# A convolution and two matmuls on one core: the start of the kernel reordered, and the two row tiles of the second matmul one sum apart

## The chip, the core and the metric

The kernel runs on one core of one Trainium2 chip. The metric is the device time of one execution in microseconds (us), the median of several runs. The engines of the core are TensorE (PE in the profile, with its weight loads as PEld), VectorE (DVE), ScalarE (ACT), GpSimd (POOL) and SyncE (SP). SP only issues DMA transfers here; POOL issues DMA transfers too.

## The reference

x is 8 rows of 4096 positions of 192 channels. Each channel belongs to one of 8 heads of 24 channels. A head has 7 weights, which go through a softmax; the output at a position is the weighted sum of that position and the six before it (zeros before the start). The result y goes through two matmuls with a leaky ReLU between them.

```python
# conv: w = softmax(weight) per head, over 7 taps
out = np.einsum('hk,bskhg->bshg', w, x_unf)      # x_unf[b,s,k] = x_pad[b, s+k]
# then, for all 32768 tokens
h = y @ w_in                    # 192 -> 2048
g = np.maximum(0.01 * h, h)
return (g @ w_out).astype(np.float32)            # 2048 -> 192
```

## The kernel before

**Tiling.** Two rows of x are worked on together: their channels lie on partitions 0 to 63 and 64 to 127, so that 192 channels are three *chunks* of 64. A *block* is 512 positions of such a pair, thus 1024 tokens; there are 32 blocks. Blocks 0 to 4 are worked on in two halves of 256 positions, which the code calls groups: groups 0 to 9 are these halves, then each of the blocks 5 to 31 is one group (list `groups`). For blocks 0 and 1 the code also counts halves of 256 positions, q = 0 to 3, which are the groups 0 to 3: "half 1" is group 1, "half 2" is group 2.

**Getting x to the engines.** For blocks 2 and up, `load_x` (L79) has POOL issue six DMA transfers that bring x to SBUF in bf16 (`x_bf`, three buffers), and `transpose_x` (L94) has SP issue three DMA transposes, one for each chunk, into `xt` (channels on partitions, positions along the row). For halves 0 to 3 the way is another: SP loads float32 (`load_first`, L110), an engine casts (`cast_first`, L128), PE transposes into PSUM (`transpose_first`, L143) and an engine copies to `xt` (`evac_first`, L157).

**Convolution.** `conv_jobs` makes 21 DVE instructions for a group: for each chunk one multiplication (L176) and six multiply-adds (L182), from `xt` into `yt`. In the first two groups TensorE does chunks 0 and 1 instead, with diagonal weight matrices (`pe_conv_jobs`, L201), and a copy scales the sum into `yt` (L317 on ACT or L207 on DVE).

**First matmul.** `mm1` (L356) fills two PSUM banks: 12 matmuls of 64 x 128 weights, chunk by chunk, the two row pairs at the same time in the two halves of the array; then one ACT instruction (L363) writes the leaky ReLU to `g`. There are two PSUM buffers (`ph`) of two banks for this. A group takes 16 calls (8 for a half block).

**Second matmul.** For each tile of 128 tokens, 16 matmul pairs add up over the 2048 features into one PSUM bank `po` (four such banks, shared with the transposes and the convolution's sums). The 128 feature rows are split in two *row tiles* of 64 rows, which run on the array at the same time but on different sums: `mm2_slot(q)` (L376) issues row tile 0 of slot q and row tile 1 of slot q - LAG, a slot being one of the 16 steps of one tile. LAG is 24 slots, one and a half sums. As both row tiles of one sum write the same bank, the first matmul of row tile 1 of a tile waits for a *seal*: a semaphore from the ACT instruction of the next `mm1` call, by which row tile 0 has left the bank. When row tile 1 ends, `evac_o` copies the sum to `o_sb` (L415; on ACT for blocks 0 to 4, on DVE after) and each second copy has SP issue the store (L418). After the last group the lone slots of row tile 1 are run, and then the last nine tiles with all 128 rows at once.

**Order.** Every queue runs in the order in which the loop at the end of the function emits instructions; nothing is rescheduled. A group has `steps` of two `mm1` calls and `quota` slots (16 slots in most steps, 8 in the steps of block 5, none in group 0); after the slots of a step come some of the convolution jobs of the *next* group (`ahead`, `per` jobs in a step). In blocks 6 and up DVE thus does, in each step, one copy and up to three jobs. `load_x(blk + 3)` and `transpose_x(blk + 2)` are emitted in the last half or the whole of a block, after a quarter and after half of its steps.

Of the kernel before, what the change touches and what calls it, by code (L numbers as in the profile page):

```python
# [9 lines left out]
FP32 = mybir.dt.float32  # L10
BF16 = mybir.dt.bfloat16
# [3 lines left out]
def kernel(  # L15
# [19 lines left out]
    CH = 64  # L35
# [5 lines left out]
    NFC = F // 128  # L41
    NB = S // ST
    NBLK = (B // 2) * NB
    LAG = NFC + NFC // 2
    WQ = 4
    NHALF = 5
    NPEC = 2
# [19 lines left out]

    x_nat, x_bf, xt = {}, {}, {}

    def load_x(blk):  # L70

        if blk >= NBLK:
            return
        rp, st = divmod(blk, NB)
        t = xb_pool.tile([128, NCH, SUB, 2, CH], BF16, name="x_bf")
        src = x[:, st * ST : (st + 1) * ST, :].rearrange("r (s p) d -> r p s d", p=128)
        for c in range(NCH):
            for e in range(2):
                nc.gpsimd.dma_start(  # L79
                    out=t[:, c, :, e, :],  # L80
                    in_=src[2 * rp + e, :, :, c * CH : (c + 1) * CH],
                )
        x_bf[blk] = t

    def transpose_x(blk):

        if blk >= NBLK:
            return
        rp, st = divmod(blk, NB)
        if st == 0:  # L90
            new_xt(rp)
        t = x_bf.pop(blk)
        for c in range(NCH):
            nc.sync.dma_start_transpose(  # L94
                out=xt[rp][:, c, HALO + st * ST : HALO + (st + 1) * ST].rearrange(
                    "p (s k) -> p s k", s=SUB
                ),
                in_=t[:, c, :, :, :].rearrange("p s e k -> p (s e k)"),
            )
# [62 lines left out]
    def conv_jobs(grp, chunks=range(NCH)):  # L162
        blk, t0, T = grp
        rp, st = divmod(blk, NB)
        if blk not in yt:
            yt[blk] = yt_pool.tile([128, NCH, ST], BF16, name="yt")
        y = yt[blk]
        jobs = []
        for c in chunks:
            for k in range(K):  # L170
                a = BASE + k + st * ST + t0
                src = xt[rp][:, c, a : a + T]
                dst = y[:, c, t0 : t0 + T]
                if k == 0:
                    jobs.append(
                        lambda s=src, d=dst, c=c: nc.vector.tensor_scalar_mul(  # L176
                            d, s, wk[:, c, 0:1]
                        )
                    )
                else:  # L180
                    jobs.append(
                        lambda s=src, d=dst, c=c, k=k: nc.vector.scalar_tensor_tensor(  # L182
                            out=d, in0=s, scalar=wk[:, c, k : k + 1], in1=d,
                            op0=mybir.AluOpType.mult, op1=mybir.AluOpType.add,
                        )
                    )
        return jobs
# [60 lines left out]
    def warm(n):  # L248
        for _ in range(n):
            nc.tensor.matmul(  # L250
                out=wa[:, 0, 0:HT], lhsT=zero[:, 0:128], rhs=zero, start=True, stop=True
            )
# [9 lines left out]
        out=w9[:, 0:K], in_=w9[:, 0:K], func=mybir.ActivationFunctionType.Exp,  # L262
        bias=nmax, scale=1.0, accum_out=w9[:, K : K + 1],
    )
    warm(7)
    wps = psum_h.tile([128, 2, ST], FP32, name="wps", tag="ph")
    for c in range(NCH):
        nc.tensor.matmul(  # L268
# [10 lines left out]
    wkh = const_pool.tile([128, NCH, K], BF16, name="wkh")  # L279
    wkl = const_pool.tile([128, NCH, K], FP32, name="wkl")  # L280
    nc.vector.tensor_copy(out=wkh, in_=wraw[:, :, 0:K])
    nc.vector.tensor_sub(wkl, wraw[:, :, 0:K], wkh)


    diag = [const_pool.tile([128, 2, K, CH], BF16, name=f"diag{c}") for c in range(NPEC)]
# [14 lines left out]
        return act  # L300

    transpose_first(0)
    warm(3)
    diag_high(0)
    diag_low(0, range(2))
    evac_first(0, nc.vector.tensor_copy, nc.scalar.copy)
# [12 lines left out]
        )  # L319

    load_first(2, low)
    for job in conv_jobs(groups[0], range(NPEC, NCH)):
        job()
    for c in range(NPEC):
        pe_jobs, evac_y = pe_conv_jobs(groups[0], c)
        for job in pe_jobs:
            job()
        evac_y(act_scale)
        warm(3)
    cast_first(1, 0, nc.vector.tensor_copy)  # L330
    cast_first(1, 1, nc.vector.tensor_copy)
    load_first(3)
    load_x(2)
    transpose_x(2)


    g, po, osb, seal = {}, {}, {}, {}
# [8 lines left out]
    def mm1(grp, u):  # L346
        blk, t0, T = grp
        y = yt[blk]
        nf = ST // T
        ph = psum_h.tile([128, 2, ST], FP32, name="ph", tag="ph")  # L350
        for i in range(nf):
            f = nf * u + i
            for c in range(NCH):
                for e in range(2):
                    ps = slice(e * CH, (e + 1) * CH)
                    nc.tensor.matmul(  # L356
                        out=ph[:, e, i * T : (i + 1) * T],
                        lhsT=w_in[ps, c, f * 128 : (f + 1) * 128],
                        rhs=y[ps, c, t0 : t0 + T],
                        start=(c == 0),  # L360
                        stop=(c == NCH - 1),
                    )
        act = nc.scalar.activation(  # L363
            out=g[blk][:, nf * u : nf * (u + 1), :, t0 : t0 + T],
            in_=ph.rearrange("p e (i t) -> p i e t", i=nf),
            func=mybir.ActivationFunctionType.Prelu, alpha=0.01,
        )
        while unsealed:
            seal[unsealed.pop()] = act.ins.name

    def mm2_one(rt, m, fc):
        b, e, s = subs[m]
# [35 lines left out]
    def evac_o(n):  # L408
# [7 lines left out]
        if n % 2 == 1:  # L416
# [3 lines left out]
                in_=osb.pop(n // 2),  # L420
            )

    slot, avail = 0, 0
    for i, grp in enumerate(groups):
        blk, t0, T = grp
        steps = T // 64
        if t0 == 0:
            g[blk] = g_pool.tile([128, NFC, 2, ST], BF16, name="g", tag="g")
        quota = (avail - slot) // steps

        if i == 0:
            ahead, pe_ahead = [], []
        elif i == 1:
            ahead = early[4:]
        else:
            ahead = conv_jobs(groups[i + 1]) if i + 1 < len(groups) else []
        per = -(-len(ahead) // (steps - 1)) if T == ST else -(-len(ahead) // steps)
        for j in range(steps):
            for u in range(2 * j, 2 * j + 2):
                mm1(grp, u)  # L440
                if i == 0 and u == 1:
                    transpose_first(1)
                    evac_first(1, nc.vector.tensor_copy, nc.vector.tensor_copy)
                    ahead = conv_jobs(groups[1], range(NPEC, NCH))
                    evacs = []
                    for c in range(NPEC):
                        pe_jobs, evac_y = pe_conv_jobs(groups[1], c)
                        pe_ahead += pe_jobs
                        evacs.append(evac_y)
                    per = len(ahead)  # L450
                if i == 0 and u == 2:
                    for e in range(2):
                        cast_first(2, e, nc.scalar.copy)
                if i == 0 and u == 4:
                    transpose_first(2)
                    evacs[0](act_scale)
                if i == 0 and u in (3, 5):
                    for job in pe_ahead[: 4 * K]:
                        job()
                    pe_ahead = pe_ahead[4 * K :]  # L460
                if i == 1 and u in (0, 2):
                    cast_first(3, u // 2, nc.scalar.copy)
            for _ in range(quota):
                mm2_slot(slot)
                slot += 1
            if i == 0 and j == 3:
                evac_first(2, nc.vector.tensor_copy, nc.vector.tensor_copy)
                early = conv_jobs(groups[2])
                for job in early[:4]:
                    job()  # L470
                evacs[1](nc.vector.tensor_scalar_mul)
# [12 lines left out]
        avail += 2 * T // 128 * NFC  # L484
    while slot < LAST * NFC + LAG:
# [36 lines left out]
```

## Time and profile before

| | us |
|---|---|
| median of 10 runs | 698.71 |
| lowest and highest run | 698.20, 700.07 |
| the profiled execution's own time | 698.33 |
| its span in the profile | 696.6 |
| TensorE matmuls busy | 690.2 |
| VectorE busy | 538.3 |
| ScalarE busy | 513.5 |
| GpSimd busy | 142.0 |

The span is what the profile covers of an execution; the execution's own time has 1.7 us more around it. The first mm1 matmul starts at 12.01; groups 1, 2, 3 and 4 start at 23.12, 34.11, 44.63 and 55.15; block 5 starts at 118.27, block 6 at 134.90, and the last step of block 31 starts at 677.52.

The lines of the timeline below have the start, then the time in us, the engine, the line of the code, the operation, output and inputs, and how many instructions are merged; in brackets is the time that the engine stood idle before, and what ended it. PE matmuls overlap each other, so that the time of a merged line runs a little past the start of the next.

### The profile page before, as it was taken

To read this page: it belongs to the slowest core of one execution; us is meant where nothing else is said; L and a number is where in the kernel's file an instruction comes from. 1 tells how busy PE (TensorE), PEld (TensorE's weight loads), DVE (VectorE), ACT (ScalarE), POOL (GpSimd) and SP (SyncE) were. 2 spreads that over 40 slices of the span, in tenths; PEclk is the share of its full clock that TensorE was granted. 3 is DMA by queue.
4 is the path that set the end of the run, shared out by engine and by line. 5 is a ranking of instruction groups with operands and counts; after the bars stand their busy time and mean duration, and the time that the engine had idled before them with its cause. 6 is when DMAs were issued, how large, how long until landed. Compare 5 with 4: busy or idle time off the path is not lost.

```text
span 696.6 us, 26058 instructions
## 1 busy us (share of the span) xinstructions
PE 690.2 (99%) x11786; PEld 613.2 (88%) x11786; DVE 538.3 (77%) x991; ACT 513.5 (74%) x579; POOL 142.0 (20%) x198
## 2 busy tenths in 40 slices
PE   9999999999999999999999999999999999999997
PEld 6899999678888888888888888888888888888887
DVE  6899999768777787777787777787777787777712
ACT  6888888977777777777777777777777777777770
POOL 6342221320222220222210222211222220000000
PEclk9999999999999999999999999999999999999999
DMA  9996554853656544556645556635556644122112
GB/s 176 123 96 79 82 78 78 88 77 75 74 66 92 82 69 82 73 67 93 81 67 81 73 70 92 81 65 84 68 76 86 85 72 70 55 52 58 47 37 69
DMA packets 184847, 54.39 MB, mean 78 GB/s; under 512 B 148384, under 2 KB 184736, under 8 KB 184736
## 3 DMA queue, kind: packets, MB, share of 16 engines
q0 software_dynamic: 98768, 14.17, 30.5%
q1 hardware_dynamic: 85968, 38.56, 23.0%
q8 instruction: 92, 1.51, 0.9%
q14 instruction: 19, 0.16, 0.1%
HBM read 29.88 MB, written 25.17 MB: 79 GB/s over the span
## 4 chain that ended last, share of the span: by engine, by line
PE 97%; DMA 1%; ACT 1%; POOL 0%; issue 0%; DVE 0%; SPq 0%; POOLq 0%; ACTq 0%
PE po L376 49%; PE ph L356 47%; DMA x_nat<-in_x_dram 1%; ACT g L363 1%; PE acc L201 0%; PE wps L268 0%; ACT diag L296 0%; POOL sel L228 0%; PE warm L250 0%; PE ptr L143 0%; ACT x_bf L128 0%; ACT xt L157 0%; POOL sel L226 0%; DVE o_sb L415 0%; POOL ident masks.py:199 0%
## 5 line engine op out<-in xcount | busy, mean ns | idle before, releaser
L363 ACT ACTIVATE g<-ph 128x1024 bf16<-128x1024 f32 x512 | 496.5, 1021 | 161.0 <-PE ph L356 161.0
L182 DVE SCALAR_TENSOR_TENSOR yt<-xt,wk,yt 128x512 bf16<-128x512 bf16 (+1 forms) x642 | 439.6, 685 | 17.4
L376 PE MATMUL po<-w_out,g 64*128 64x192 bf16 (+1 forms) x8048 | 398.0, 243 | 0.1
L376 PEld LDWEIGHTS <-g 64*128 64x128 bf16 (+1 forms) x8048 | 372.1, 94 | 29.0 <-ACT g L363 0.4
L356 PE MATMUL ph<-yt,w_in 64*128 64x512 bf16 (+1 forms) x3552 | 391.7, 347 | 1.4 <-ACT g L363 1.1
L356 PEld LDWEIGHTS <-w_in 64*128 64x128 bf16 x3552 | 250.0, 94 | 45.8 <-issue 4.8
L79 POOL DMA_DIRECT2D x_bf<-in_x_dram x180 | 133.7, 773 | 431.1 <-DMA xt<-x_bf 422.7
L415 DVE COPY o_sb<-po 128x192 f32<-128x192 f32 x216 | 77.2, 357 | 129.6 <-PE po L376 127.2
L176 DVE TENSOR_SCALAR yt<-xt,wk 128x512 bf16<-128x512 bf16 (+1 forms) x107 | 35.9, 336 | 1.0 <-DMA xt<-x_bf 0.7
L415 ACT COPY o_sb<-po 128x192 f32<-128x192 f32 x40 | 13.1, 327 | 0.0
L201 PE MATMUL acc<-xt,diag 64*64 64x256 bf16 x112 | 8.2, 303 | 0.0
L201 PEld LDWEIGHTS <-diag 64*64 64x64 bf16 x112 | 6.6, 121 | 1.5 <-issue 0.4
L250 PE MATMUL warm<-zero 128*128 128x256 bf16 x20 | 4.5, 373 | 1.1 <-DVE junk L218 1.1
L238 POOL DMA_DIRECT2D w_in<-in_moe_w_in_dram x8 | 5.1, 643 | 0.0
L157 DVE COPY xt<-ptr 128x384 bf16<-128x384 bf16 x7 | 2.2, 352 | 3.2 <-PE ptr L143 3.2
L128 ACT CAST x_bf<-x_nat 128x384 bf16<-128x384 f32 x5 | 2.5, 506 | 2.5 <-DMA x_nat<-in_x_dram 2.5
L250 PEld LDWEIGHTS <-zero 128*128 128x128 bf16 x20 | 2.0, 122 | 2.2 <-DVE junk L218 1.1
L296 ACT ACTIVATE diag<-ident,wkl 128x64 bf16<-128x64 bf16 x14 | 3.6, 337 | 0.1
L317 ACT ACTIVATE yt<-acc,rsum 128x256 bf16<-128x256 f32 x3 | 1.4, 474 | 2.0 <-PE acc L201 2.0
L128 DVE CAST x_bf<-x_nat 128x384 bf16<-128x384 f32 x3 | 1.4, 488 | 1.4 <-DMA x_nat<-in_x_dram 1.4
L268 PEld LDWEIGHTS wps<-w,sel 8*128 8x128 f32 x6 | 1.3, 320 | 0.7 <-POOL sel L228 0.7
L255 ACT ACT_TABLE_LOAD x1 | 1.3, 1283 | 0.8 <-PEq L506 0.8
(28 smaller groups left out, 12.5 us busy)
## 6 DMA issues: line engine op xcount, KB each, us to landing
out_dram<-o_sb SPq DMA_DIRECT2D x128, 192.0 KB, 2.1
x_bf<-in_x_dram POOLq DMA_DIRECT2D x180, 64.0 KB, 3.2
x_nat<-in_x_dram SPq DMA_DIRECT2D x8, 192.0 KB, 5.0
w_in<-in_moe_w_in_dram POOLq DMA_DIRECT2D x8, 192.0 KB, 8.9
xt<-x_bf SPq DMA_TRANSPOSE x90, 2.5
w_out<-in_moe_w_out_dram POOLq DMA_DIRECT2D x1, 768.0 KB, 14.5
w<-in_weight_dram SPq DMA_DIRECT2D x1, 0.2 KB
```

The costliest lines, as they stand in the source:

```text
L79: nc.gpsimd.dma_start(out=t[:, c, :, e, :], in_=src[2 * rp + e, :, :, c * CH : (c + 1) * CH],)
L128: copy(out=x_bf[q // 2][:, :, h * HS : (h + 1) * HS, e, :], in_=x_nat[q][:, e, :, :].rearrange("p s (c k) -> p c s k", c=NCH),)
L176: lambda s=src, d=dst, c=c: nc.vector.tensor_scalar_mul(d, s, wk[:, c, 0:1])
L182: lambda s=src, d=dst, c=c, k=k: nc.vector.scalar_tensor_tensor(out=d, in0=s, scalar=wk[:, c, k : k + 1], in1=d, op0=mybir.AluOpType.mult, ...
L201: lambda k=k, p=p, a=a, e=e, ps=ps: nc.tensor.matmul(out=acc[ps, :T], lhsT=diag[c][ps, p, k, :], rhs=xt[0][ps, c, a : a + T], start=(k == ...
L238: nc.gpsimd.dma_start(out=w_in[e * CH : (e + 1) * CH, :, fs], in_=moe_w_in[:, fs].rearrange("(c p) f -> p c f", p=CH),)
L250: nc.tensor.matmul(out=wa[:, 0, 0:HT], lhsT=zero[:, 0:128], rhs=zero, start=True, stop=True)
L296: act = nc.scalar.activation(out=diag[c][:, 1, k, :], in_=ident2, func=mybir.ActivationFunctionType.Copy, scale=wkl[:, c, k : k + 1],)
L356: nc.tensor.matmul(out=ph[:, e, i * T : (i + 1) * T], lhsT=w_in[ps, c, f * 128 : (f + 1) * 128], rhs=y[ps, c, t0 : t0 + T], start=(c == 0) ...
L363: act = nc.scalar.activation(out=g[blk][:, nf * u : nf * (u + 1), :, t0 : t0 + T], in_=ph.rearrange("p e (i t) -> p i e t", i=nf), func=my ...
L376: ins = nc.tensor.matmul(out=po[m], lhsT=g[b][ps, fc, e, s * 128 : (s + 1) * 128], rhs=w_out[ps, fc, :], start=(rt != 1 and fc == 0), stop ...
L415: copy(out=o_sb[:, n % 2, :], in_=po.pop(n))
```

## The change

The change has these parts:

- **LAG** becomes 16 slots, exactly one sum. The seal is no longer the ACT instruction: the first matmul of the next `mm1` call releases a memset of one element on POOL (`ptoken`), and this memset releases row tile 1.
- **POOL's queue**: `load_x` no longer issues its six transfers at once but puts them in a list; each step takes one from it, or two in half blocks. `load_x(blk + 3)` is called in the first step of the block. `transpose_x(blk + 2)` is called in the step before the last.
- **Block 2**: its load moves from the start to step 1 of group 1, behind the load of block 3, which is called a step earlier; its transposes move from the start to step 0 of group 3.
- **Half 1**: its casts go between the convolution jobs of group 0, and its transposes and copies ahead of the first mm1 matmul. Of its convolution, TensorE does chunk 0 alone, and DVE chunks 1 and 2.
- **Half 2** is cast on DVE instead of ACT, and transposed at the end of group 0. The copies of half 3 come after step 1 of group 1 instead of step 3.
- The warm-up matmuls are 8, 4, 4 and 2 instead of 7, 4, 3, 3 and 3, and two small weight tables hold two chunks instead of three.

```diff
-    LAG = NFC + NFC // 2
+    LAG = NFC
...
 def load_x(blk):
...
-                nc.gpsimd.dma_start(
-                    out=t[:, c, :, e, :],
-                    in_=src[2 * rp + e, :, :, c * CH : (c + 1) * CH],
+                loads.append(
+                    lambda c=c, e=e: nc.gpsimd.dma_start(
+                        out=t[:, c, :, e, :],
+                        in_=src[2 * rp + e, :, :, c * CH : (c + 1) * CH],
+                    )
                 )
...
-    warm(7)
+    warm(8)
...
-    warm(3)
+    warm(4)
...
-    for job in conv_jobs(groups[0], range(NPEC, NCH)):
+    for n, job in enumerate(conv_jobs(groups[0], range(NPEC, NCH))):
+        if n in (4, 5):
+            cast_first(1, n - 4, nc.vector.tensor_copy)
         job()
+    load_first(3)
     for c in range(NPEC):
...
-        warm(3)
-    cast_first(1, 0, nc.vector.tensor_copy)
-    cast_first(1, 1, nc.vector.tensor_copy)
-    load_first(3)
-    load_x(2)
-    transpose_x(2)
+        if c == 0:
+            warm(2)
+    transpose_first(1)
+    evac_first(1, nc.vector.tensor_copy, nc.vector.tensor_copy)
...
 def mm1(grp, u):
...
+                    if unsealed:
+
+                        token = nc.gpsimd.memset(ptoken, 0.0)
+                        tc.add_manual_dep(
+                            token.ins, ins.ins.name,
...
+                        while unsealed:
+                            seal[unsealed.pop()] = token.ins.name
...
-        while unsealed:
-            seal[unsealed.pop()] = act.ins.name
...
         if i == 0:
-            ahead, pe_ahead = [], []
-        elif i == 1:
-            ahead = early[4:]
+            ahead = []
...
-                if i == 0 and u == 1:
-                    transpose_first(1)
-                    evac_first(1, nc.vector.tensor_copy, nc.vector.tensor_copy)
-                    ahead = conv_jobs(groups[1], range(NPEC, NCH))
-                    evacs = []
-                    for c in range(NPEC):
-                        pe_jobs, evac_y = pe_conv_jobs(groups[1], c)
-                        pe_ahead += pe_jobs
-                        evacs.append(evac_y)
+                if i == 0 and u == 0:
+                    pe_ahead, evac_y = pe_conv_jobs(groups[1], 0)
+                    ahead = conv_jobs(groups[1], range(1, NCH))
                     per = len(ahead)
-                if i == 0 and u == 2:
-                    for e in range(2):
-                        cast_first(2, e, nc.scalar.copy)
-                if i == 0 and u == 4:
-                    transpose_first(2)
-                    evacs[0](act_scale)
-                if i == 0 and u in (3, 5):
-                    for job in pe_ahead[: 4 * K]:
+                if i == 0 and u == 3:
+                    for job in pe_ahead:
                         job()
-                    pe_ahead = pe_ahead[4 * K :]
...
             if i == 0 and j == 3:
+                evac_y(nc.vector.tensor_scalar_mul)
+                for e in range(2):
+                    cast_first(2, e, nc.vector.tensor_copy)
+                transpose_first(2)
                 evac_first(2, nc.vector.tensor_copy, nc.vector.tensor_copy)
-                early = conv_jobs(groups[2])
-                for job in early[:4]:
-                    job()
-                evacs[1](nc.vector.tensor_scalar_mul)
+            if i == 1 and j == 1:
+
+                nc.gpsimd.tensor_copy(out=pjunk, in_=g[0][0:1, NFC - 1, 1, HT - 1 : HT])
+                load_x(2)
+            if i == 3 and j == 0:
+                transpose_x(2)
             for job in ahead[per * j : per * (j + 1)]:
                 job()
             if i == 1 and j == 1:
                 transpose_first(3)
-            if i == 1 and j == 3:
                 evac_first(3, nc.vector.tensor_copy, nc.vector.tensor_copy)
...
-            if j == steps // 4 and last_half:
+            if j == 0 and last_half:
                 load_x(blk + 3)
-            if j == steps // 2 and last_half and blk > 0:
+            if loads:
+                loads.pop(0)()
+            if loads and T < ST:
+                loads.pop(0)()
+            if j == steps - 2 and last_half and blk > 0:
                 transpose_x(blk + 2)
```

More of the change, by code (lines that the diff above doesn't have):

```diff
@@ L68 @@
     x_nat, x_bf, xt = {}, {}, {}
+    loads = []
     def load_x(blk):
@@ L278 @@
     wraw = wps[:, 0, 0 : NCH * (K + 1)].rearrange("p (c k) -> p c k", c=NCH)
[L279 to L282, printed above, removed]
+    wkh = const_pool.tile([128, NPEC, K], BF16, name="wkh")
+    wkl = const_pool.tile([128, NPEC, K], FP32, name="wkl")
+    nc.vector.tensor_copy(out=wkh, in_=wraw[:, 0:NPEC, 0:K])
+    nc.vector.tensor_sub(wkl, wraw[:, 0:NPEC, 0:K], wkh)
     diag = [const_pool.tile([128, 2, K, CH], BF16, name=f"diag{c}") for c in range(NPEC)]
@@ L355, in mm1 @@
                     ps = slice(e * CH, (e + 1) * CH)
-                    nc.tensor.matmul(
+                    ins = nc.tensor.matmul(
                         out=ph[:, e, i * T : (i + 1) * T],
@@ L362, in mm1 @@
                     )
-        act = nc.scalar.activation(
+                    if unsealed:
+                        token = nc.gpsimd.memset(ptoken, 0.0)
+                        tc.add_manual_dep(
+                            token.ins, ins.ins.name,
+                            mybir.DependencyInfo(
+                                mybir.DependencyClass.Sync, mybir.DependencyReason.DATA
+                            ),
+                            reason="row tile 0 has left its bank",
+                        )
+                        while unsealed:
+                            seal[unsealed.pop()] = token.ins.name
+        nc.scalar.activation(
             out=g[blk][:, nf * u : nf * (u + 1), :, t0 : t0 + T],
@@ L421, in evac_o @@
             )
+    pjunk = const_pool.tile([1, 1], BF16)
+    ptoken = const_pool.tile([1, 1], FP32)
     slot, avail = 0, 0
```

## The prediction, made before the changed kernel ran

> **What bounds the kernel now.** I read the page's first part, then the chain that ended last.
>
> ```profile
> span 696.6 us, 26058 instructions
> PE 690.2 (99%) x11786; PEld 613.2 (88%) x11786; DVE 538.3 (77%) x991; ACT 513.5 (74%) x579; POOL 142.0 (20%) x198
> PE 97%; DMA 1%; ACT 1%; POOL 0%; issue 0%; DVE 0%; SPq 0%; POOLq 0%; ACTq 0%
> ```
>
> TensorE sets the end from the first matmul on. DVE's 77% is an average over two regimes, so I went on to the timeline, at three places. First the arrival of `w_out` and the two queues beside it:
>
> ```profile
> 24.25 3.70 POOL L79 DMA_DIRECT2D x_bf<-in_x_dram  x5 [3.68 <-DMA w_out<-in_moe_w_out_dram]
> ...
> 24.88 3.99 SPq L94 DMA_TRANSPOSE xt<-x_bf  x3
> ```
>
> `w_out` is in at about 24.2; the first mm2 matmul starts at 24.68, just behind it. Block 2 is transposed by SP from 24.88. Then groups 3 and 4:
>
> ```profile
> 39.78 10.89 SPq L418 DMA_DIRECT2D out_dram<-o_sb  x3
> 40.38 0.43 DVE L176 TENSOR_SCALAR yt<-xt,wk 128x256 bf16<-128x256 bf16 x1
> ...
> 43.85 0.28 DVE L176 TENSOR_SCALAR yt<-xt,wk 128x256 bf16<-128x256 bf16 x1
> ...
> 44.63 1.49 PE L356 MATMUL ph<-yt,w_in 64*128 64x256 bf16 x24
> ...
> 47.18 0.28 DVE L176 TENSOR_SCALAR yt<-xt,wk 128x256 bf16<-128x256 bf16 x1
> ...
> 50.50 0.28 DVE L176 TENSOR_SCALAR yt<-xt,wk 128x256 bf16<-128x256 bf16 x1
> 50.78 4.67 SPq L94 DMA_TRANSPOSE xt<-x_bf  x3
> ...
> 55.15 1.05 PE L356 MATMUL ph<-yt,w_in 64*128 64x256 bf16 x16
> ```
>
> Group 4's convolution runs on DVE from 40.38 to 50.50, a chunk each 3.32 us; PE starts group 3 at 44.63 and group 4 at 55.15. So DVE leads PE by 4.65 us and has almost no idle time here: 9.97 us of jobs in a period of 10.52. SP's transposes stand behind output stores. Last, a whole block and the tail:
>
> ```profile
> 215.75 0.36 DVE L415 COPY o_sb<-po 128x192 f32<-128x192 f32 x1
> 216.02 2.31 DVE L182 SCALAR_TENSOR_TENSOR yt<-xt,wk,yt 128x512 bf16<-128x512 bf16 x3
> ...
> 218.74 1.53 PE L356 MATMUL ph<-yt,w_in 64*128 64x512 bf16 x12
> ```
>
> ```profile
> 678.90 14.13 PE L376 MATMUL po<-w_out,g 64*128 64x192 bf16 x168
> ...
> 680.96 11.83 PEld L376 LDWEIGHTS <-g 128*128 128x128 bf16 x144 [0.16 <-issue]
> ```
>
> In a whole block the last convolution job ends 0.41 us before PE's next block (216.02 + 2.31 against 218.74). In the tail 24 slots, 16 paired and 8 of row tile 1 alone, take 1.98 us (678.90 to about 680.88): 0.082 us a slot.
>
> [...] convolution matmul pairs are 0.21 us apart up to 9.28 and 0.12 after 9.92[...] a transpose lands 2.4 us after its issue when alone, 3.3 to 4.1 behind an output store, 6.0 to 6.6 among `x_bf` loads (those at 24.88).
>
> **The change, part by part.**
>
> *Start.* The warm-ups net to two fewer between the two PE convolutions and the first mm1: 8 and 4 in place of 7 and 3 before the convolutions, where PE waits for POOL's `sel` and DVE's `xt` anyway (0.0 to +0.2 us), then 2 in place of 3, then none (about 0.11 us each at full clock, as a convolution pair then takes). The 12 transposes of half 1 (0.35) move before mm1; there PE otherwise waits for ACT's second y copy (11.69 + 0.47). DVE's two casts (0.96) go between group 0's jobs, so its chunk ends at 11.7 rather than 10.8, still before that copy. First ACT on g: 12.97 becomes about 12.8. Group 0 is then paced by ACT's 8 activations at 0.985: one PE convolution (1.65) instead of two, 0.35 of transposes, and no casts on ACT (1.0). `w_in` is in by about 19.3 (11.9 us after its last issue at 7.4), so its last quarter holds mm1 slightly. Group 1 starts at about 21.2 instead of 23.12. DVE's extra chunk (7 jobs, 3.32) and two casts (0.96) end at 20.4, in time. But mm2 then stands at 22.8 before `w_out`, which all 16 DMA engines, busy since 3 us, deliver at 24.2 as before; `x_bf` loads queue behind it, so deferring them frees little. Of 2 us won, **0.5 is kept** (bounds: nothing, and 1.2 if `w_out` is early). Steps of 2.9, 2.69, 2.63 follow: group 2 at 33.6 (was 34.11), group 3 at 44.1 (44.63). DVE: half 2's copies end at 21.6, 12 jobs to 27.3, waiting for half 3's transposes on PE to 28.4, then 0.62 and 9 jobs: group 2 is convolved at 33.4, just in time; group 3 at 43.4.
>
> *Block 2's transposes* move from the start to step 0 of group 3, behind the slots of that step and thus on SP behind the output store of pair (6, 7). With LAG 16 tile 7's sum ends with the last slot of that step. So: 44.1 + 2.63 (step) + 0.2 (as from PE to a copy in the tail) + 0.33 (ACT copy, L415) + 0.03 + 0.48 (store to transpose at 50.3 and 50.78) = 47.8 for the issue. POOL's block 4 loads, two a step, run in the same 8 us. Landing: bounds 2.4 and 6.6; I take **4.5**, above the 3.3 to 4.1 behind a store alone. DVE, idle since 43.4, begins group 4 at 52.4 and ends 3 × 3.32 later at 62.3. All of DVE's queue is behind that wait, with groups 5 to 9 and block 5. PE reaches group 4 at 54.6 and chunk 2 of its first bank at 54.8: **it waits about 7.5 us**. Had the transposes landed by 44.9, it would wait nothing.
>
> *Lost lead.* From here DVE has no lead. In the trace before it needs 65.1 us from 50.50 to the end of block 5's convolution at 115.6 (5 groups, 50.1, and 3 chunks of 4.99); PE needs 63.1 from group 4 (55.15) to block 5 (118.27). So block 5 is convolved at 127.4, while PE would ask for its chunk 2 at 62.1 + 63.1 + 0.43 = 125.6: **1.8 us more**. Block 5 then counts as started at 127.0 instead of 118.27: **+8.7**. Block 6's convolution (15.0) fits into block 5 (16.6). [...]
>
> *LAG 24 to 16.* The lone tail of 8 slots goes: 8 × 0.082 = **−0.66**. The lone slots of row tile 0 at the start cost nothing either way, as they are slots of the same number. Copies to `o_sb` come half a step (0.66) later. On DVE the last convolution job of a whole block then ends 0.25 after PE's next block start, but chunk 2 is read only 0.43 after it. Left are 0.18, or about 0.1 past a semaphore: taken as 0, bounds 0 and +2.5 (0.1 × 25 blocks). Transposes at step 6 land some 23 us into a block and are needed at 24.1.
>
> *The token.* PE's first mm1 matmul of a step (0.38) releases a 1x1 memset on POOL (0.1, like its start-up memsets) which releases row tile 1 after both mm1 units (1.31): about 0.7 us with 0.1 per hop[...]. POOL's loads (0.74 each, one or two a step) come after the step's token and end before the next. `x_bf` buffers are long transposed, so POOL is not held there. Cost 0; without this cover, every 0.1 us past 1.31 is paid in some 245 steps.
>
> Sum: 8.7 − 0.66 = **+8.0** on the profiled execution's 698.33 (span 696.6, so 1.7 outside it), which is 0.38 under the median shown. As a median: 698.71 + 8.0 = **706.7**.
>
> **Rivals.**
> *Block 2 is in time (not slower).* Place: SP's queue. If the transposes went as soon as the loads (ended in step 1 of group 2, about 40) have landed, DVE would run on from 43.4 to 53.4, 1.2 us ahead of PE; block 5 would cost 0.2. Then −0.5 − 0.66 + 0.2: 697.7. For it: x is loaded early enough, and DVE is free. Against: SP issues in order, and the store ahead needs a sum that ends at 46.7. It decides at a landing of 44.9, three us before the issue can happen.
> *The convolution's tail is late in every whole block.* If the last job ends 0.2 us past its margin, PE waits 0.2 × 25 = 5: 711.7. For it: only 0.1 us of room. Against: jobs of 2.31 to 2.32 per step are very steady.
> *The token is late.* At 1.4 us it costs 0.1 × 245 = 25: 731. Against: 0.6 us of slack and a POOL that is 20% busy.
>
> **How the numbers follow.** Stall at block 2: 0.83, its own range 703.8 (landing 2.4, a better start) to 710.5 (6.6, clock, some tail). Block 2 in time: 0.05. Late tail: 0.08. Late token: 0.04. The range runs from 703.5 to 711.5: it leaves out block 2 in time, the token, most of the late tail and a twentieth of the first case. 0.2% (1.4 us) is about what a measurement of this kernel tells from no change. Block 2 in time gives −0.14%, a little better with an early `w_out`: same 0.03, faster 0.02. The rest is slower: 0.95.
>
> **What would show it.** After: a wait of DVE's L176 for the transposed `xt` of 8 to 9 us near 43; PE idle before mm1 near 55 to 62, for DVE, and again near 125; transposes with SP's fourth store just ahead; first mm2 near 24.2; no lone slots in the tail; block periods of 20.9 as before. Wrong would be: no such wait of DVE, a period above 21.0 in whole blocks, or PE waits for POOL.

## The result and the profile after

The changed kernel takes 704.88 us (median of 8 runs, 704.36 to 706.07), the kernel before 698.74 (29 runs). The ratio is 1.0089, with a 95% interval of 1.0080 to 1.0098: 6.1 us slower. The profiled execution has a span of 703.4 (703.45 unrounded), 6.83 more than before. 706.7 was predicted, with a range of 703.5 to 711.5.

In three of the comparisons below (one store earlier, the start alone, the parts together) the ratio stands nearer to 1 than the medians do: of the kernels that start as the changed one, some executions take 1.6 to 4.7 us more at a mean TensorE clock of 0.995 to 0.998, and the ratios, unlike the medians, take these in.

The page of the changed kernel, first part and the chain by engine:

```profile
span 703.4 us, 26493 instructions
PE 689.4 (98%) x11756; PEld 547.8 (78%) x11756; DVE 549.3 (78%) x1000; ACT 516.5 (73%) x576; POOL 164.2 (23%) x446
...
PE 91%; DVE 4%; DMA 4%; ACT 1%; issue 0%; POOL 0%; SPq 0%; POOLq 0%
```

PE is busy for about as long as before (690.2), but no longer for the whole span: its share of the chain fell from 97% to 91%, and 4% each are now with DVE and with transfers. The view of waits says which (engine, what it waited to do, for whom: us in total, times, longest):

```profile
POOL ptoken L370 <- PE ph L361: 452.8, 247, 13.1
...
PE ph L361 <- DVE yt L186: 7.3, 4, 3.0
```

PE waits for DVE's convolution four times, 7.3 us in all, and nowhere for POOL: the token waits for PE, not PE for the token. The timeline of the changed kernel, at the arrival of `w_out` and from the store of tiles 6 and 7 to the end of the wait:

```profile
23.90 1.31 PE L391 MATMUL po<-w_out,g 64*128 64x192 bf16 x14 [0.34 <-DMA w_out<-in_moe_w_out_dram]
...
43.73 1.54 PE L361 MATMUL ph<-yt,w_in 64*128 64x256 bf16 x24
...
46.98 0.37 SPq L433 DMA_DIRECT2D out_dram<-o_sb  x1
47.47 3.92 SPq L98 DMA_TRANSPOSE xt<-x_bf  x3
...
51.73 0.29 DVE L180 TENSOR_SCALAR yt<-xt,wk 128x256 bf16<-128x256 bf16 x1 [8.69 <-DMA xt<-x_bf]
...
55.20 0.28 PE L361 MATMUL ph<-yt,w_in 64*128 64x256 bf16 x2 [0.72 <-DVE yt L186]
58.52 0.40 PE L361 MATMUL ph<-yt,w_in 64*128 64x256 bf16 x2 [3.04 <-DVE yt L186]
...
61.84 2.31 PE L361 MATMUL ph<-yt,w_in 64*128 64x256 bf16 x20 [2.92 <-DVE yt L186]
63.92 2.12 PE L391 MATMUL po<-w_out,g 64*128 64x192 bf16 x32
```

Block 2's transposes are issued half a us after the store and land 4.3 us later; DVE has stood idle for 8.69 us by then. PE takes DVE's chunks one by one and waits 6.68 us for the three (0.72 + 3.04 + 2.92). 20 matmuls then take 2.31 us and 32 of the second matmul 2.12, against 1.27 and 1.50 at full speed (an experiment below has them): PE is at half clock (the granted clock in the trace is 0.50 from 58.4 to 65.1 and 1.00 from 65.2 on), and comes to the next step at 65.86, 4.02 us after 61.84 instead of 2.41. The next wait for DVE is at block 5. The timeline there, DVE's first job for block 6, and PE's first matmul of block 6:

```profile
126.36 0.60 PE L361 MATMUL ph<-yt,w_in 64*128 64x512 bf16 x4
...
127.41 0.35 DVE L180 TENSOR_SCALAR yt<-xt,wk 128x512 bf16<-128x512 bf16 x1
127.55 1.04 PE L361 MATMUL ph<-yt,w_in 64*128 64x512 bf16 x8 [0.59 <-DVE yt L186]
...
143.75 1.48 PE L361 MATMUL ph<-yt,w_in 64*128 64x512 bf16 x12
```

In a whole block (the same stretch of a block as shown of before) and in the tail:

```profile
225.31 2.32 DVE L186 SCALAR_TENSOR_TENSOR yt<-xt,wk,yt 128x512 bf16<-128x512 bf16 x3
225.31 0.09 POOL L370 MEMSET ptoken<- 1x1 f32 x1 [2.52 <-PE ph L361]
...
227.43 1.47 PE L361 MATMUL ph<-yt,w_in 64*128 64x512 bf16 x12
...
686.37 13.47 PE L391 MATMUL po<-w_out,g 64*128 64x192 bf16 x160
```

The last convolution job ends at 227.63, 0.20 after the first matmul of PE's next block, without a wait. The token, released by the step that began at 224.81, is there 0.59 after it. In the tail 16 slots come where there were 24 (160 and 168 matmuls in the line, 144 of them the last nine tiles).

Where the 6.83 us come from is seen when the span is cut at the start of block 6, where PE runs without a wait in both kernels (143.75 and 134.90):

| | before | after | difference |
|---|---|---|---|
| start to block 6 | 134.90 | 143.75 | +8.85 |
| block 6 to the first matmul of the last step | 542.62 | 541.30 | -1.32 |
| the last step and the tail | 19.10 | 18.40 | -0.70 |

So there is one loss, ahead of block 6, and two gains after it, one of which (-1.32) the prediction did not have.

### The profile page after: what moved, and what is told of

Same layout as the page of the kernel before. It is cut to its first block, busy times and chain, and to the rows that moved or that the text cites. A ratio compares the mean times of both kernels' runs of the same rounds, so it can differ in the third digit from the quotient of the medians.

```text
span 703.4 us, 26493 instructions
## 1 busy us (share of the span) xinstructions
PE 689.4 (98%) x11756; PEld 547.8 (78%) x11756; DVE 549.3 (78%) x1000; ACT 516.5 (73%) x576; POOL 164.2 (23%) x446
## 4 chain that ended last, share of the span: by engine, by line
PE 91%; DVE 4%; DMA 4%; ACT 1%; issue 0%; POOL 0%; SPq 0%; POOLq 0%
PE po L391 46%; PE ph L361 44%; DVE yt L186 3%; DMA w_out<-in_moe_w_out_dram 2%; ACT g L380 1%; DMA w_in<-in_moe_w_in_dram 1%; DMA xt<-x_bf 1%; DVE yt L180 0%; POOL sel L232 0%; SPq L433 0%; POOL sel L230 0%; DVE o_sb L430 0%; ACT o_sb L430 0%; POOL ident masks.py:199 0%; POOL ident masks.py:197 0%
## 5 line engine op out<-in xcount | busy, mean ns | idle before, releaser
L186 DVE SCALAR_TENSOR_TENSOR yt<-xt,wk,yt 128x512 bf16<-128x512 bf16 (+1 forms) x648 | 442.4, 683 | 17.6
L391 PEld LDWEIGHTS <-g 64*128 64x128 bf16 (+1 forms) x8048 | 355.6, 94 | 45.2 <-issue 0.7
L361 PE MATMUL ph<-yt,w_in 64*128 64x512 bf16 (+1 forms) x3552 | 381.7, 348 | 8.9 <-DVE yt L186 7.3
L391 PE MATMUL po<-w_out,g 64*128 64x192 bf16 (+1 forms) x8048 | 385.7, 243 | 0.3 <-DMA w_out<-in_moe_w_out_dram 0.3
L361 PEld LDWEIGHTS <-w_in 64*128 64x128 bf16 x3552 | 191.5, 94 | 101.7 <-issue 10.8
L370 POOL MEMSET ptoken<- 1x1 f32 x247 | 21.9, 89 | 452.8 <-PE ph L361 452.8
L180 DVE TENSOR_SCALAR yt<-xt,wk 128x512 bf16<-128x512 bf16 (+1 forms) x108 | 44.1, 408 | 9.6 <-DMA xt<-x_bf 9.4
L205 PE MATMUL acc<-xt,diag 64*64 64x256 bf16 x84 | 6.7, 321 | 0.0
```

Of the source, the lines that this page charges most:

```text
L180: lambda s=src, d=dst, c=c: nc.vector.tensor_scalar_mul(d, s, wk[:, c, 0:1])
L205: lambda k=k, p=p, a=a, e=e, ps=ps: nc.tensor.matmul(out=acc[ps, :T], lhsT=diag[c][ps, p, k, :], rhs=xt[0][ps, c, a : a + T], start=(k == ...
L361: ins = nc.tensor.matmul(out=ph[:, e, i * T : (i + 1) * T], lhsT=w_in[ps, c, f * 128 : (f + 1) * 128], rhs=y[ps, c, t0 : t0 + T], start=(c ...
L370: token = nc.gpsimd.memset(ptoken, 0.0)
L391: ins = nc.tensor.matmul(out=po[m], lhsT=g[b][ps, fc, e, s * 128 : (s + 1) * 128], rhs=w_out[ps, fc, :], start=(rt != 1 and fc == 0), stop ...
```

## The experiments

My theory after the result: block 2's late transposes are the loss; PE is late at block 6 because DVE is late, by whatever DVE was kept waiting. The token as seal gives the 1.32 and LAG the tail. The rivals: DVE had too much to do between groups 4 and 9 with or without the wait; the start or the whole blocks lose something that the late block 2 covers.

### Block 2 early

```diff
-            if i == 1 and j == 1:
-
-                nc.gpsimd.tensor_copy(out=pjunk, in_=g[0][0:1, NFC - 1, 1, HT - 1 : HT])
+            if i == 1 and j == 0:
                 load_x(2)
-            if i == 3 and j == 0:
+            if i == 1 and j == 3:
                 transpose_x(2)
...
-            if j == 0 and last_half:
+            if j == (1 if i == 1 else 0) and last_half:
+                if i == 1:
+                    nc.gpsimd.tensor_copy(out=pjunk, in_=g[0][0:1, NFC - 1, 1, HT - 1 : HT])
                 load_x(blk + 3)
```

Block 2's load now goes ahead of block 3's, and its transposes go into the last step of group 1. The copy into `pjunk` moves along, to stand ahead of the second of the two loads, as before.

> The changed kernel, but block 2 is loaded ahead of block 3 and its transposes are issued in the last step of group 1 (about 33 us), ahead of the stores of groups 1 and 2. Theory (block 2's late transposes are the whole loss, and the rest of the change gains): DVE's wait of 8.7 us goes, groups 4 to 9 run without a wait of PE, block 5 counts as started at about 117.6 (0.7 to 0.9 before the kernel before), and the 1.3 of the whole blocks and 0.7 of the tail stay gained: 704.9 - 9.5 = 695.4, below the kernel before. Rival (DVE lacks the capacity in groups 4 to 9 with or without the wait, so block 5 is late anyway): DVE is idle less, PE waits near block 5 for about 1 to 2 us, 697 to 700. Rival (the loss is elsewhere): 704.9, unchanged.

Measured: 696.63 us (695.66 to 697.27), ratio to the kernel before 0.9968 (0.9956 to 0.9980), span 695.0. Its timeline at SP, and PE at block 5:

```profile
31.70 0.39 SPq L433 DMA_DIRECT2D out_dram<-o_sb  x1
32.20 3.91 SPq L98 DMA_TRANSPOSE xt<-x_bf  x3
```

```profile
119.14 1.04 PE L361 MATMUL ph<-yt,w_in 64*128 64x512 bf16 x8 [0.60 <-DVE yt L186]
```

DVE begins group 4 at 43.46 without a wait, and 8.4 us of the loss are gone (block 6 starts at 135.33 instead of 143.75): the earlier place of block 2's load and transposes turns the change from 0.9% slower to 0.3% faster. But I had expected 695.4; block 6 still starts 0.43 later than in the kernel before. Block 5 takes 17.46 us on PE instead of 16.63, as PE waits there for DVE, which convolves one more chunk of half 1 than before (7 jobs, 3.32 us). So there is something in the rival that DVE lacks capacity, 0.8 us of it. The extra chunk alone doesn't make this wait: the last experiment has it too, and loses 0.1 us there.

### The transposes one store earlier

```diff
-            if i == 3 and j == 0:
+            if i == 2 and j == 2:
                 transpose_x(2)
```

> The changed kernel with block 2's transposes issued in step 2 of group 2, one output store earlier in SP's queue (behind the store of tiles 4 and 5 instead of 6 and 7), about 5.3 us earlier. Theory (every us by which they are late past what DVE has in hand is paid by PE): DVE's wait falls from 8.7 to about 3.4, PE's wait at group 4 from 6.7 to about 1.5, its wait at block 5 is about 1.8 as the lead is still lost, and no half clock comes: block 5 counts as started at 127.1 - 5.3 = 121.8, median about 699.5. Rival (the transposes land with the loads of block 4 and not by their issue): DVE's wait stays near 8 and the median at 704.9.

Measured: 697.92 us (696.72 to 701.61), ratio 0.9998 (0.9985 to 1.0010), span 696.0; block 6 starts at 136.30. Its timeline:

```profile
42.60 3.94 SPq L98 DMA_TRANSPOSE xt<-x_bf  x3
...
45.14 0.29 DVE L180 TENSOR_SCALAR yt<-xt,wk 128x256 bf16<-128x256 bf16 x1 [1.70 <-DMA xt<-x_bf]
```

Issued 4.87 us earlier, they land in 2.5 us rather than 4.3, so that DVE goes on 6.59 us earlier; half of my expected wait is left. Group 4 then takes PE only 0.4 us more than 10.52. The lead is lost all the same and is paid at block 5: PE waits 1.35 us there, where the changed kernel has 0.59. That the transposes are held by their place in SP's queue, and not by the loads, is shown.

### Does the half clock cost anything?

```diff
         quota = (avail - slot) // steps
+        if i == 4:
+            wa = psum_h.tile([128, 2, ST], FP32, name="warm2", tag="ph")
+            warm(64)
```

> The changed kernel with 64 warm-up matmuls on PE ahead of group 4, so that PE keeps its clock through most of the wait for block 2. Theory (what the half clock costs in group 4 is covered by block 5's wait, because DVE sets when block 5 can start): group 4 runs at full clock and block 5's wait grows from 0.8 to about 2.1, the median stays at 704.9 within 0.4. Rival (the half clock is paid in full): 703.5.

Measured: 705.28 us (704.59 to 708.85), span 703.8. PE in its timeline:

```profile
55.14 7.16 PE L254 MATMUL warm<-zero 128*128 128x256 bf16 x64
...
63.03 1.27 PE L361 MATMUL ph<-yt,w_in 64*128 64x256 bf16 x20 [0.41 <-DVE yt L186]
64.12 1.50 PE L391 MATMUL po<-w_out,g 64*128 64x192 bf16 x32
```

The same 20 and 32 matmuls now take 1.27 and 1.50 us, so the clock was kept (0.995 is the mean granted clock of the changed kernel's profiled execution, 1.0 of this one); at block 5 PE's wait shows 1.35 us instead of 0.59 (I had expected it to grow more, from 0.8 to 2.1), and the time is no better. The 1.6 us at half clock (4.02 less the 2.41 from 63.03 to the next step at 65.44) were covered: block 6 could not start earlier in any case. In this execution the transposes landed 1.2 us later than in the changed kernel (DVE goes on at 52.93), so the two times alone would prove little. What decides is in one table, of the kernels of this and the other experiments in which the timeline has a wait of PE at block 5 ("DVE starts on block 6" is its first multiplication for that block, right behind the convolution of block 5):

| | DVE goes on with group 4 | DVE starts on block 6 | PE starts block 6 | difference of the last two |
|---|---|---|---|---|
| changed kernel | 51.73 | 127.41 | 143.75 | 16.34 |
| warm-ups in the wait | 52.93 | 127.76 | 144.09 | 16.33 |
| one store earlier | 45.14 | 119.97 | 136.30 | 16.33 |
| block 2 early | 43.46 | 119.00 | 135.33 | 16.33 |
| start alone (next) | 43.02 | 118.14 | 134.47 | 16.33 |

Whatever PE lost or gained before, block 6 starts on PE 16.33 us after DVE has ended block 5's convolution and taken up the next. In the kernel before, where PE doesn't wait there, it is 18.49 (116.41 to 134.90). So in these kernels DVE alone sets it.

### The start alone

Halves 1 to 3 and the warm-ups of the changed kernel, everything else as before (LAG 24, ACT seal, loads at once, block 2 at the start):

```diff
...
     evac_first(1, nc.vector.tensor_copy, nc.vector.tensor_copy)
+    load_x(2)
+    transpose_x(2)
...
```

This is against the changed kernel; the lines that take LAG, seal and loads back to the kernel before are left out.

> The start of the changed kernel (halves 1 to 3, warm-ups) on the kernel before: LAG 24, the ACT seal, six loads at once, block 2 loaded and transposed at the start. Theory (w_out's arrival holds the first mm2, so of the 2 us won before it little is kept): group 2 starts 0.5 to 0.9 earlier than before and the lead is kept to the end: median 697.8 to 698.2. Rival (without the hold): 2 us earlier, 696.7. Rival (the start gains nothing, its 0.9 in the changed kernel came from the missing block 2 loads): 698.7.

Measured: 698.05 us (median of 21, 697.10 to 702.77), ratio 1.0001 (0.9990 to 1.0013): no difference that can be told. In the profiled execution the first mm2 matmul starts at 23.61, again held by `w_out`, group 4 at 54.01, 1.14 before the kernel before; 0.7 of this is lost in the wait for DVE at block 5, and block 6 starts 0.43 earlier. The same kernel once more:

> The start of the changed kernel on the kernel before, once more. Before, 6 of its 21 executions took 2 to 4.5 us longer, at a mean clock of 0.995 to 0.998. Theory (TensorE's clock is halved for a stretch in the first 25 us, where it is idle more than in the kernel before): if this execution is one of those, a slice of PEclk ahead of 35 us stands below 10 besides the first. If not, the median's 698.0 and a span of 695.9 come again.

Measured: 697.35 us, span 695.6. In this one group 4 starts at 54.22, PE loses 0.3 at block 5, and block 6 starts 0.66 earlier than before. Six of the 21 executions took 2.2 to 4.7 us over the median with a clock of 0.995 to 0.998, none of the 27 of the next two kernels, which start as before. The kernel before is not quite free of it: one of the 13 executions that ran beside the last experiment took 701.25 at 0.998. No execution of that kind was profiled; in which stretch the clock falls there is open, and so is whether the new start causes it.

### Token and LAG without the start

The start and block 2 of the kernel before, with the token, one load a step and the later transposes; once with LAG 16 and once with LAG 24. The first edit is against the kernel before and leaves out what is as in the change; the second takes the LAG 16 kernel to LAG 24:

```diff
...
     load_x(2)
+    while loads:
+        loads.pop(0)()
     transpose_x(2)
...
```

```diff
-    LAG = NFC
+    LAG = NFC + NFC // 2
```

> The start and block 2 of the kernel before, with the rest of the change: LAG 16, the token on POOL as seal, one load a step, transposes in the step before the last. Theory (the ACT seal came 0.04 us late in the first step of each whole block, and the tail has eight lone slots less): blocks 6 to 31 take 541.3 instead of 542.6, the tail 18.35 instead of 19.08, median 698.7 - 1.3 - 0.7 = 696.7. Rival (the whole blocks differ by what the late block 2 left behind, not by the seal): only the tail gains, 698.0.

> As the run with the rest of the change on the start of the kernel before, but LAG 24. Theory (the 1.3 us of the whole blocks come from the token, the 0.7 of the tail from LAG): blocks 6 to 31 take 541.3, the tail 19.1, median 697.4. Rival (the 1.3 us come from the later copies of LAG 16): blocks take 542.6 and the median is 698.7.

Measured: 697.14 us with LAG 16 (696.63 to 697.93, ratio 0.9980, 0.9971 to 0.9989) and 697.36 with LAG 24 (696.65 to 698.65, ratio 0.9983, 0.9976 to 0.9991). Spans 695.1 and 695.7. From block 9 on, a block takes 20.92 us in all these kernels with the token, at either LAG, and 20.96 in the two with the ACT seal (start alone, and the kernel before but for one block). So the token gives the gain in the whole blocks. These kernels differ in how the loads are spread too, but the LAG 24 kernel of the next experiment has the token alone, and its last two blocks before block 31, in which POOL issues no loads, also take 20.92; in the kernel before the same two take 20.96. The timeline of the kernel before shows where it had been: the second matmul of the first step of a block, and that of the next step.

```profile
219.73 1.94 ACT L363 ACTIVATE g<-ph 128x1024 bf16<-128x1024 f32 x2 [0.74 <-PE ph L356]
220.04 1.60 PE L376 MATMUL po<-w_out,g 64*128 64x192 bf16 x32
...
222.69 1.56 PE L376 MATMUL po<-w_out,g 64*128 64x192 bf16 x32
```

With LAG 24 row tile 1 turns to a new tile in the middle of the step. Its matmuls, merged in the line, start 0.08 us apart, the last of the old tile at 220.70, so that the first of the new one was due at 220.78. The first of the two ACT instructions (1.02 us, as all of them) ends at 220.75, and the matmul starts at 220.81. The step takes 2.65 us (220.04 to 222.69), the other seven of the block 2.61 or 2.62; with the token at LAG 24 this step takes 2.61 or 2.62 too. In all, from block 6 to the end: 561.41 with ACT seal and LAG 24 (start alone), 560.46 with the token and LAG 24, 559.70 to 559.71 with the token and LAG 16. Token 0.95, LAG 0.76, of which 0.66 are the lone slots of the tail and 0.10 come in block 6, the first whole block. (With LAG 16 the figure is that of the changed kernel and of the last experiment; the LAG 16 kernel here has 560.10.) The kernel before has 561.72; 0.28 of its difference to the start alone are one single block that took 21.24.

LAG 16 had a price of its own here that the changed kernel hides. The waits of DVE and of PE in the LAG 16 kernel, around block 6:

```profile
DVE yt L180 <- DMA xt<-x_bf: 5.3, 1, 5.3
```

```profile
PE ph L362 <- DVE yt L186: 0.2, 1, 0.2
```

Block 6's transposes are again behind a store: SP issues them at 116.81, with LAG 24 at 114.26. Block 6 takes 21.31 us instead of 20.92, which is the 0.4 between 560.10 and 559.70: the mistake of block 2 in small.

### A token behind six loads

The kernel before with the token as seal, but with the six loads of a block at once, with LAG 16 and with LAG 24:

```diff
+                    if unsealed:
+                        token = nc.gpsimd.memset(ptoken, 0.0)
...
-        while unsealed:
-            seal[unsealed.pop()] = act.ins.name
```

> The kernel before with the token as seal and LAG 16, but the six loads of a block still issued at once. Theory (a token that stands behind POOL's loads is late, and each 0.1 us of it is paid): after the loads, 6 x 0.74 = 4.45 us, the next step's token comes at about 5.1 us after the step of the loads started, and row tile 1 wants it at 2.62 + 1.31 = 3.93: 1.2 us late once a block, 27 x 1.2 = 32, less the 2.0 of the seal and the tail: about 729. Rival (POOL's issue runs ahead and does not hold the token): 696.7.

> As the run with the token, LAG 16 and loads at once, but LAG 24. There row tile 1's first slot of a tile is half a step later, so the token is wanted at 2.62 + 1.97 = 4.59 and comes at 5.1: 0.5 late once a block, 27 x 0.5 = 14, less the 1.3 of the seal: about 711. Rival (no hold): 697.4.

Measured: 743.15 us with LAG 16 (743.06 to 743.47, ratio 1.0635, 1.0620 to 1.0649) and 724.67 with LAG 24 (724.31 to 725.24, ratio 1.0370, 1.0356 to 1.0384). The LAG 16 kernel, waits and timeline:

```profile
PE po L386 <- POOL ptoken L365: 40.8, 28, 1.5
```

```profile
194.24 0.09 POOL L365 MEMSET ptoken<- 1x1 f32 x1 [2.53 <-PE ph L356]
194.84 4.46 POOL L79 DMA_DIRECT2D x_bf<-in_x_dram  x6 [0.51 <-issue]
...
196.36 1.53 PE L356 MATMUL ph<-yt,w_in 64*128 64x512 bf16 x12
...
199.24 0.09 POOL L365 MEMSET ptoken<- 1x1 f32 x1
199.39 1.49 PE L386 MATMUL po<-w_out,g 64*128 64x192 bf16 x31 [1.49 <-POOL ptoken L365]
```

The mechanism is as expected, the delay larger: 0.51 us pass between a token and the first load, which I had left out, so that the next token ends at 199.33, 5.6 after the step of the loads began (193.75) and not 5.1. A block then takes 22.58 us with LAG 16 and 21.92 with LAG 24: 1.66 and 1.00 more than 20.92, and the two differ by 0.66, the half step by which LAG 24 asks later. The loads are spread over the steps for this reason: without that the token costs 45 us.

### The parts together

The changed kernel with block 2 loaded and transposed at the start as before, and the transposes of blocks 3 to 6 one store earlier; and the same with the start of the kernel before:

```diff
...
-            if j == steps - 2 and last_half and blk > 0:
+            if j == (steps - 2 if T == ST else 1) and last_half and blk > 0:
                 transpose_x(blk + 2)
```

> The changed kernel with block 2 loaded and transposed at the start as in the kernel before, and with the transposes of the blocks 3 to 6 one step (one output store) earlier. Theory (the parts add up: start 0.4 with block 5 waiting about 0.7 for DVE, token 1.3, tail 0.7): block 5 starts at 117.8, blocks take 20.92, the tail 18.4: span 694.2, median 695.9, below the run with block 2 early (696.63) as half 3's copies hold DVE less. Rival (the start's lead is lost at block 5 anyway, so it is worth nothing): as with the old start, 696.7.

> The start of the kernel before with token, spread loads and LAG 16, and the transposes of the blocks 3 to 6 one output store earlier. Theory (in the run with the same but late transposes DVE waits 5.25 us for block 6's transposes and PE 0.45 at block 6): the wait goes, block 6 starts at 135.0, span 694.7, median 696.6. Rival (that wait costs nothing): 697.1.

Measured: 695.88 us with the new start (695.51 to 698.79, ratio 0.9971, 0.9957 to 0.9984, span 694.1), 696.44 with the old (696.27 to 696.82, ratio 0.9967, 0.9955 to 0.9979, span 694.6). The page of the one with the new start:

```profile
span 694.1 us, 26499 instructions
PE 687.0 (99%) x11756; PEld 549.2 (79%) x11756; DVE 548.5 (79%) x1000; ACT 516.3 (74%) x576; POOL 163.8 (24%) x445
...
PE 95%; DMA 3%; ACT 1%; POOL 0%; issue 0%; DVE 0%; POOLq 0%
```

The parts add up to within 0.1 to 0.2 us of what was expected, and DVE is gone from the chain: contrary to my expectation, PE loses only 0.1 us at block 5 in this execution (it takes 16.73 us instead of 16.63), too little to show as a wait. Block 6 still starts 16.34 after DVE's turn to it, so DVE sets it here too, but only just. At group 4 DVE leads PE by 11.29 us here and in block 2 early, which lost 0.8; what differs is DVE's way from there to the end of block 5's convolution, 74.9 us here and 75.6 there. The last section has the reason. Both beat the kernel before. The intervals of the two overlap, so which start is better isn't settled; 3 of 8 executions with the new start have a clock of 0.997 or 0.998 and take 1.6 to 2.9 us over the median, none of 5 with the old (one of 13 of the kernel before, as said above). Once more with the new start:

> The best kernel with the new start once more. Of its 8 executions 3 took 1.6 to 2.9 us over the median, at a mean clock of 0.997 or 0.998. Theory (with the new start TensorE's clock is sometimes halved for a stretch ahead of block 5): if this execution is one of those, PEclk stands below 9 in a slice ahead of 120 us and the span is 696 to 697. If not, the span of 694.1 comes again.

Measured: 695.50 us, span 693.8, at full clock (a mean of 1.0). It says nothing on the open question.

## Why the prediction was right

The forecast of slower, and the place and kind of the loss, were right. Step by step:

- **Start, "0.5 is kept".** 0.9 was: groups 2 and 3 started at 33.21 and 43.73, not at 33.6 and 44.1. `w_out` held the first mm2 matmul as foreseen, but at 23.90 and not 24.2. In the eight profiled executions with this start, all held by `w_out`, it starts between 23.6 and 24.6, and group 2 started between 32.97 and 33.94, so the size of this term isn't known better than by 0.5.
- **Block 2's transposes.** Issue at 47.8 predicted, 47.47 measured; landing 4.5 against 4.3; DVE goes on at 52.4 against 51.73; PE waits "about 7.5" against 6.68. Taking the issue out of its place behind the store takes the loss away.
- **Lost lead.** Block 5 was to count as started at 127.0; it is 143.75 - 16.63 = 127.12. That this is so close is luck in part: DVE went on 0.7 earlier than forecast, and its way to the end of block 5's convolution took 75.77 us and not 75.0, as DVE's multiplications took longer where they started during POOL's issue of a load (7.03 us for the 21, and 6.19 with the warm-ups; last section). The two errors cancel. The prediction took this way over from the trace before and did not ask what the spread loads would do to it; there one such job already took 0.47 (at 121.40). PE's wait there was smaller than the 1.8 of the prediction (about 0.8), because the half clock had already taken 1.6 us of PE's time: the one came out of the other, and the prediction's sum rightly has no term for the half clock. With the warm-ups it waits about 1.5.
- **LAG.** The tail was to win 0.66; it is 0.70 in the two traces and 0.66 between the two kernels that differ in LAG alone. All 24 slots of the tail before are of row tile 1 alone (168 matmuls less 144), and not 16 paired and 8 alone, as the prediction read them; the price of 8 slots is the same. The end of the last convolution job, 0.25 after PE's next block in the prediction, is at 0.20, and no block waits. The rival of a late tail is out.
- **Token.** There 0.59 us after the step's start, where 0.7 was predicted; no wait of PE on POOL. Its rival, that every 0.1 us past 1.31 is paid, is right as a mechanism: where the token is late, all of it is paid (with LAG 16 and six loads at once, 40.8 us of waits, and 45 us of time).
- **The step that failed** is "Cost 0" for the seal. It asked only what the new seal might cost, and not whether the old one was late. The whole blocks gave 1.32 us: 0.95 by the token, 0.3 by an odd block in the profiled execution of before, and 0.1 by LAG. The forecast of +8.0 and the 6.83 of the spans differ by 1.2: these 1.32, less the 0.15 that block 6 came later than forecast (8.85 against 8.7). The 0.4 gained beyond the forecast at the start doesn't enter the sum, because DVE and not PE sets the start of block 6.
- **Block 2 in time**, the rival at 697.7, was tried as block 2 early: 696.63. Its 0.2 us at block 5 were 0.8, but it lacked the token's 0.95 too.

## What to carry to other kernels

When a change moves a DMA issue, look first at what stands ahead of it on the same queue: an output store waits for a sum, and everything behind it waits too, here DVE stood idle for 8.7 us before three transposes whose data had landed by 40.5, 7 us ahead of their issue. If the engine that this starves has a lead of a few us and no spare capacity, the loss goes one to one to the end, and extra cost elsewhere before that point (here 1.6 us at half clock) is free. For a new semaphore, price the old one as well: a wait that is on time in most steps can be late in one of each block.

## What the runs showed of the hardware

- **Most of DVE's `TENSOR_SCALAR` jobs that started while POOL was issuing a load took longer.** A multiplication on a whole block takes 0.35 us otherwise. Of the changed kernel:

```profile
152.54 0.74 POOL L82 DMA_DIRECT2D x_bf<-in_x_dram  x1 [0.36 <-issue]
152.75 0.63 DVE L180 TENSOR_SCALAR yt<-xt,wk 128x512 bf16<-128x512 bf16 x1
```

  It ends 0.1 us after the issue does. From 44 us on, 37 of the changed kernel's 99 such jobs start during an issue, and 34 of these take longer than any of the other 62 (0.353 at most); in two of the remaining three (at 132.40 and 403.78) it is POOL's issue that is longer, 0.82 and 0.85 us instead of 0.74. The third, on a half block, starts 0.62 us into an issue (at 78.58) and keeps its 0.28; so does one on a whole block in the kernel before, also 0.62 us into an issue (at 100.61), with 0.35. The multiply-adds (L186) keep their 0.48 and 0.75, the 108 that start during an issue too. Spread loads meet more of these jobs than the bursts of the kernel before, where 4 of 97 start in an issue; the mean of all multiplications is 0.41 us in the changed kernel and 0.34 in the kernel before. DVE's way from group 4 to the end of block 5's convolution varies with it, between 74.8 and 75.7 us in the table above: its 21 multiplications take 7.03 us in the changed kernel and 6.19 with the warm-ups, its 126 multiply-adds 65.89 in both. In block 2 early the multiplications take 6.90, and 6.13 in the last kernel with the new start.
- **The clock fell during a wait of 3.04 us**: the granted clock is still 1.00 up to 58.3, about 2.8 us after the two matmuls at 55.20 have ended, and 0.50 from 58.4 on; the two matmuls at 58.52 already take 0.40 instead of 0.28. Full speed is back at 65.2, 3.4 us after PE is busy again at 61.84.
- **A token on POOL is quick**: from the start of a step's first matmul to the end of its memset 0.59 us (224.81 to 225.40 in the changed kernel), in a step that has 1.31 for it.
